# W_Q's load in two parts, of 16 and of 112 partitions, in a decode step on one core

## The chip, the cores and the metric

The kernel runs on one core of a Trainium2 chip. The metric is the device time of one execution in microseconds. Beside it there is the profile of one execution, taken by the hardware profiler: a span from the first to the last instruction, the busy time of each engine, and the packets that the core's 16 DMA engines moved. Engines are named as the profile names them: PE (TensorE's matmuls), PEld (its weight loads), DVE (VectorE), ACT (ScalarE), POOL (GpSimd), SP (SyncE, which only issues DMAs and waits here). SPq and ACTq are the DMA issues of SP and ACT.

## The reference

One decode step: four tokens (batch 4, one position, width 512) go through a layernorm and then, in parallel, through a sliding window attention over a cache and through a gated feed-forward block. All inputs are bf16.

```
xn = layernorm(x)                                   # 4 x 512
q  = xn @ wq                                        # 32 heads of 128
k, v = the last 4096 positions of the caches        # 8 key heads, each for 4 query heads
a  = softmax(q k^T / sqrt(128)) v @ wo
b  = (silu(xn @ w_gate) * (xn @ w_up)) @ w_down     # 1792 wide
out = x + a + b
```

The keys and values that are read make 32 MB each, W_Q and W_O 4 MB each, and the three matrices of the feed-forward block 1.75 MB each: 81.01 MB in all for one step of four tokens.

## The kernel before, in words

The program is written out by hand, engine by engine, with semaphores between the engines; nothing is planned by a scheduler.

**Loads.** SP issues nearly all of them, in one fixed order (L240 to L254): W_Q (L240), the keys of units 0 and 1 (`load_k`, L226), W_gate (L243), W_up (L244), the values of unit 0 (`load_v`, L230), then keys and values in turn, W_down (L249), the last values in two halves (L234), and W_O in five pieces (L238). A unit is one key head for two of the four batch rows: 4096 positions twice over, 2 MB of keys and 2 MB of values, so there are 16 units. Every load that SP issues into the chip's memory goes over 128 partitions: W_Q as 128 rows of 32 KB, a unit of keys as 128 rows of 16 KB. The loads of W_Q, keys 0 and 1, W_gate and W_up wait for nothing; the values of unit d wait until PE has finished with the values of the unit before (`s_pv`, L229), and the keys of unit d until unit d - 2 has been transposed (`s_tr`, L225). Two buffers stand for the keys and two for the values. ACT issues the load of x (L258), 4 rows of 1 KB.

**Start.** ACT and DVE make the layernorm from x; PE transposes it (L361) and DVE copies it out (L283). PE then waits for W_Q on the semaphore `d_wq` (L365) and computes q in 32 matmuls (L372, which stand in the profile under the helper's line, L356). They take W_Q by column blocks: every one of them reads all 128 partitions. DVE transposes q (L286) and spreads it out for the units (L289).

**Loop.** Eight passes over two units each (L432). In each half PE waits for the keys (`d_k`, L437), transposes them in groups of eight blocks (L384), and DVE copies each group out of PSUM (L298); PE multiplies them with q (L394), a row maximum is taken and subtracted (L303, L308, L404), ACT takes the exponential (L269), and PE multiplies with the values (L418). DVE normalizes the result (L312).

**End.** After the loop PE computes the feed-forward block's two first products (L454), the last values, the product with W_down (L466), and the product with W_O, piece by piece as its five loads land (L176). The result is copied out by DVE and ACT (L488, L490) and stored by SP (L492).

A load increments its semaphore by 16 when all of it has landed. Two loads on one semaphore are both complete at 32.

Of the kernel before, what the change touches and what calls it, by code (L numbers as in the profile page):

```python
# [10 lines left out]
def bass_parallel_sum__sliding_block_cached__swiglu_ffn__decode_kernel(  # L11
# [10 lines left out]
    out: bass.AP,  # L22
):
    B, _, D = A_x.shape
    _, HKV, Sk, Dh = A_k_cache.shape
    HQ = A_wq.shape[1] // Dh
    F = B_w_gate.shape[1]
# [25 lines left out]
    WQ = sb("wq_sb", [128, NC * HQ * Dh], BF16)  # L53
# [58 lines left out]
    def sem(name):  # L112
        return nc.alloc_semaphore(name=name)
    d_x = sem("d_x")
    d_wq = sem("d_wq")
# [44 lines left out]
    wq_ap = A_wq.rearrange("(p c) n -> p (c n)", c=NC)  # L160
# [6 lines left out]
    def kv_ap(cache, d):  # L167
        b0 = d % 2 * 2
        return cache[b0:b0 + 2, d // 2, Sk - W:, :].rearrange("b (q t) d -> q b (t d)", t=NT)
# [10 lines left out]
    with nc.Block() as block:  # L180
# [40 lines left out]
        @block.sync  # L221
        def _(eng):
            def load_k(d):
                if d >= 2:
                    eng.wait_ge(s_tr, 2 * NG * (d - 1))  # L225
                eng.dma_start(KB[:, d % 2 * KVN:(d % 2 + 1) * KVN], kv_ap(A_k_cache, d)).then_inc(d_k[d % 2], 16)  # L226

            def load_v(d):
                eng.wait_ge(s_pv, d + 1)  # L229
                eng.dma_start(VB[:, d % 2 * KVN:(d % 2 + 1) * KVN], kv_ap(A_v_cache, d)).then_inc(d_v[d % 2], 16)  # L230

            def load_v_half(d, h, done):
                a = d % 2 * KVN + h * HKN
                eng.dma_start(VB[:, a:a + HKN], kv_ap(A_v_cache, d)[:, :, h * HKN:(h + 1) * HKN]).then_inc(done, 16)  # L234

            def load_wo(n):
                a, b = WO_CUTS[n], WO_CUTS[n + 1]
                eng.dma_start(WO[:, a:b, :], wo_ap[:, a:b, :]).then_inc(d_wo[n], 16)  # L238

            eng.dma_start(WQ[:], wq_ap).then_inc(d_wq, 16)  # L240
            load_k(0)
            load_k(1)
            eng.dma_start(WG[:], wg_ap).then_inc(d_wg, 16)  # L243
            eng.dma_start(WU[:], wu_ap).then_inc(d_wu, 16)  # L244
            load_v(0)
            for d in range(2, ND):
                load_k(d)
                load_v(d - 1)
            eng.dma_start(WD[:], wd_ap).then_inc(d_wd, 16)  # L249
            eng.wait_ge(s_pv, ND)  # L250
            load_v_half(ND - 1, 0, d_v[1])
            load_v_half(ND - 1, 1, d_vz)
            for n in range(len(d_wo)):
                load_wo(n)  # L254
# [99 lines left out]
        def _(eng):  # L354
# [7 lines left out]
                                     xn[:].rearrange("b (p c) -> b c p", c=NC)[:, c, :], I4[:])  # L362
            last.then_inc(s_xT, 1)
            eng.wait_ge(s_xnT, 1)
            eng.wait_ge(d_wq, 16)  # L365

            for n in range(2):
                for c in range(NC):
# [153 lines left out]
```

## Time and profile before

| what | value |
|---|---|
| median of three runs | 196.37 us (196.15 to 196.51) |
| the profiled execution | 196.04 us |
| its span, first to last instruction | 194.8 us |
| mean granted clock of TensorE | 0.991 |
| bytes moved, mean rate over the span | 81.10 MB, 416 GB/s |
| busy time of PE, PEld, DVE, ACT, POOL | 162.8, 140.4, 114.9, 17.0, 10.3 us |
| W_Q from its issue to its landing | 12.4 us |

The busy times overlap, since the engines work side by side, and a busy PE is not a PE at its peak. "Idle before" in a row is the time an engine waited ahead of a group of instructions, with what ended it. The chain that ended last follows the work back from the last instruction, at each step to what released it. A window row gives the window, its length, the busy time of PE, PEld, DVE, ACT and POOL in it with the number of instructions, the granted clock, the share of time that the 16 DMA engines were busy, and the rate in GB/s; bytes count in the window in which their packet starts.

### The profile page before, as it was taken

The numbers are of one execution on the slowest core, as the hardware profiler recorded it, in microseconds if no ns is written. First come the engines' busy times: TensorE is split into PE (matmuls) and PEld (weight loads), VectorE is DVE, ScalarE is ACT, GpSimd is POOL, SyncE is SP. The second block draws the span as 40 slices with busy tenths as digits, with TensorE's granted clock in tenths as the row PEclk, the third lists the DMA queues.
The fourth block names the chain that finished last, engine by engine and source line by source line (L and its number), as shares of the span: only waits on it lengthen the run. The fifth ranks groups of instructions, "written<-read, shape, count | busy, mean of one in ns | idle before, by whom it ended". The sixth has DMA issues, their size and how long they took to land.

```text
span 194.8 us, 7757 instructions
## 1 busy us (share of the span) xinstructions
PE 162.8 (84%) x3465; PEld 140.4 (72%) x3466; DVE 114.9 (59%) x250; ACT 17.0 (9%) x27; POOL 10.3 (5%) x23
## 2 busy tenths in 40 slices
PE   0127999379898989898989898989898989898995
PEld 0113898378887888788878887888788878886752
DVE  1004777237676767676767676767676767675610
ACT  6600101001010101010101010101010101010100
POOL 8930000000000000000000000000000000000000
PEclk9999999879999999999999999999999999999999
DMA  6999999999999999999999999999999999999992
GB/s 216 431 431 431 434 421 434 422 431 431 431 431 431 434 427 431 434 431 434 434 431 431 431 431 434 431 431 431 431 431 431 431 431 431 431 433 417 439 401 105
DMA packets 6070, 81.10 MB, mean 416 GB/s; under 512 B 680, under 2 KB 816, under 8 KB 1072
## 3 DMA queue, kind: packets, MB, share of 16 engines
q1 hardware_dynamic: 6056, 81.01, 97.7%
q8 instruction: 5, 0.08, 0.1%
q14 instruction: 1, 0.01, 0.0%
q10 hardware_dynamic: 8, 0.00, 0.0%
HBM read 81.01 MB, written 0.00 MB: 416 GB/s over the span
## 4 chain that ended last, share of the span: by engine, by line
DMA 63%; PE 32%; issue 1%; DVE 1%; SPq 1%; DVEq 0%
DMA kbuf<-in_A_k_cache_dram 48%; PE ps_kt L384 16%; DMA wo_sb<-in_A_wo_dram 9%; PE ps_s L356 8%; DMA wq_sb<-in_A_wq_dram 6%; PE ps_o L356 5%; PE ps_kt L356 2%; PE ps_acc L176 1%; PE ps_acc L356 1%; DVE kT L298 1%; SPq L234 1%; DVE kT L286 0%; SPq L238 0%; DVE y_sb L488 0%; DVE qz L289 0%
## 5 line engine op out<-in xcount | busy, mean ns | idle before, releaser
L298 DVE COPY kT<-ps_kt 128x1024 bf16<-128x1024 bf16 x128 | 79.5, 684 | 24.8 <-PE ps_kt L384 24.8
L384 PE MATMUL ps_kt<-ident,kbuf 128*128 128x128 bf16 x1024 | 62.7, 219 | 10.2 <-DMA kbuf<-in_A_k_cache_dram 10.2
L384 PEld LDWEIGHTS ps_kt<-ident,kbuf 128*128 128x128 bf16 x1024 | 57.3, 98 | 15.3 <-issue 15.3
L356 PE MATMUL ps_o<-p,vbuf 128*128 128x64 bf16 x1120 | 39.2, 195 | 0.0
L356 PEld LDWEIGHTS ps_o<-p,vbuf 128*128 128x128 bf16 x1120 | 36.0, 99 | 1.1
L356 PEld LDWEIGHTS ps_s<-qz,kT 128*128 128x128 bf16 x1024 | 32.0, 99 | 6.7 <-issue 3.6
L356 PE MATMUL ps_s<-qz,kT 128*128 x1024 | 35.3, 193 | 1.2
L303 DVE TENSOR_REDUCE rm<-ps_s 128x8 bf16<-128x512 f32 x17 | 11.8, 692 | 23.9 <-PE ps_s L356 23.9
L269 ACT ACTIVATE p<-ps_s 128x512 bf16<-128x512 f32 x17 | 10.2, 597 | 162.4 <-PE ps_s L356 162.4
L356 PE MATMUL ps_o<-p,ones 128*128 128x128 bf16 (+1 forms) x69 | 7.0, 224 | 4.5 <-DMA vbuf<-in_A_v_cache_dram 3.1
L356 PEld LDWEIGHTS ps_o<-p,ones 128*128 128x128 bf16 x69 | 4.6, 99 | 5.6 <-DMA vbuf<-in_A_v_cache_dram 3.3
L356 PE MATMUL ps_kt<-wq_sb,xnT 128*32 128x512 bf16 x32 | 3.6, 629 | 5.7 <-DMA wq_sb<-in_A_wq_dram 5.7
L356 PE MATMUL ps_s<-dg,ones 8*128 8x512 bf16 x17 | 6.5, 385 | 0.0
L356 PE MATMUL ps_s<-mkc,mkr 2*128 2x512 bf16 x17 | 6.5, 385 | 0.0
L361 PE MATMUL ps_acc<-i,xn 4*128 4x4 f32 x4 | 0.6, 254 | 7.0 <-ACT xn L266 7.0
L356 PEld LDWEIGHTS ps_kt<-wq_sb,xnT 128*32 128x32 bf16 x32 | 1.2, 138 | 7.2 <-issue 7.2
L286 DVE STREAM_TRANSPOSE kT<-ps_kt 128x512 f32<-128x512 f32 x2 | 1.4, 718 | 8.4 <-PE ps_kt L356 8.4
L361 PEld LDWEIGHTS ps_acc<-i,xn 4*128 4x128 f32 x4 | 0.6, 206 | 7.0 <-issue 7.0
L314 DVE TENSOR_REDUCE den<-ps_o 128x8 f32<-128x128 f32 x18 | 4.9, 274 | 1.0 <-PE ps_o L356 1.0
L216 POOL MEMSET vbuf<- 128x6144 f32 x1 | 5.2, 5223 | 0.0
L308 DVE TENSOR_REDUCE m<-ps_acc 8x1 f32<-8x128 f32 x17 | 4.6, 270 | 0.3 <-PE ps_acc L356 0.3
L318 DVE TENSOR_TENSOR oT<-ps_o,den 128x8 f32 (+1 forms) x18 | 3.0, 167 | 2.9 <-issue 2.7
(68 smaller groups left out, 50.1 us busy)
## 6 DMA issues: line engine op xcount, KB each, us to landing
kbuf<-in_A_k_cache_dram SPq DMA_DIRECT2D x16, 2048.0 KB, 12.6
vbuf<-in_A_v_cache_dram SPq DMA_DIRECT2D x15, 2048.0 KB, 11.3
wq_sb<-in_A_wq_dram SPq DMA_DIRECT2D x1, 4096.0 KB, 12.4
vbuf<-in_A_v_cache_dram SPq DMA_DIRECT2D x2, 1024.0 KB, 9.2
wo_sb<-in_A_wo_dram SPq DMA_DIRECT2D x1, 2048.0 KB, 14.6
wg_sb<-in_B_w_gate_dram SPq DMA_DIRECT2D x1, 1792.0 KB, 25.7
wu_sb<-in_B_w_up_dram SPq DMA_DIRECT2D x1, 1792.0 KB, 29.3
wd_sb<-in_B_w_down_dram SPq DMA_DIRECT2D x1, 1792.0 KB, 15.0
```

What stands on the lines that cost most here:

```text
L176: last = eng.matmul(ps_acc[64 * n:64 * n + B, 0:256], OP[:, c, :], WO[:, c, 256 * n:256 * n + 256], start=False, stop=True, skip_group_che ...
L216: eng.memset(VB[:, HKN:].bitcast(FP32), 0.0)
L234: eng.dma_start(VB[:, a:a + HKN], kv_ap(A_v_cache, d)[:, :, h * HKN:(h + 1) * HKN]).then_inc(done, 16)
L269: eng.activation(P[:, d % 2 * PS:d % 2 * PS + SN], ps_S[d % 2][:], ACT.Exp, scale=SCALE).then_inc(s_p, 1)
L286: eng.transpose(qT[:, 512 * n:512 * n + 512], ps_kt[n][:])
L298: eng.tensor_copy(KT[:, u * HKN + 1024 * g:u * HKN + 1024 * (g + 1)], kt_ps[g].rearrange("p a b -> p (a b)")).then_inc(s_ev, 1)
L303: eng.tensor_reduce(RM[:], ps_S[bank][:].rearrange("p (t c) -> p c t", c=C), AX.X, ALU.max).then_inc(s_rm, 1)
L308: eng.tensor_reduce(m8[:], mt_ps, AX.X, ALU.max)
L314: eng.tensor_reduce(den[:], den_ps.rearrange("p (t c) -> p c t", c=C), AX.X, ALU.add)
L318: eng.tensor_tensor(OT[:, 2 * b:2 * b + 2, ds(r * REP, REP)], O_ps.rearrange("p (j h) -> p j h", j=2), den[:].rearrange("p (j h) -> p j h" ...
L356: return eng.matmul(o, l, r, start=start, stop=stop, skip_group_check=True)
L384: last = eng.transpose(kt_ps[g][:, k, :], KB[:, a:a + 128], ident[:])
```

## The change

W_Q comes in two loads, the first into partitions 0 to 15, the second into partitions 16 to 127. Both are issued by SP, one behind the other, at the place of the one load, and both increment `d_wq`, so PE waits for 32 in place of 16. Source rows, destination rows and everything else stay as they were; lines behind the load move down by two.

```diff
-            eng.dma_start(WQ[:], wq_ap).then_inc(d_wq, 16)
+
+            eng.dma_start(WQ[0:16, :], wq_ap[0:16, :]).then_inc(d_wq, 16)
+            eng.dma_start(WQ[16:128, :], wq_ap[16:128, :]).then_inc(d_wq, 16)
             load_k(0)
             load_k(1)
             eng.dma_start(WG[:], wg_ap).then_inc(d_wg, 16)
...
             eng.wait_ge(s_xnT, 1)
-            eng.wait_ge(d_wq, 16)
+            eng.wait_ge(d_wq, 32)
```

## The prediction

> **What bounds the kernel now.** I read the page first, from its slices down to the chain that ended last.
>
> ```profile
> span 194.8 us, 7757 instructions
> ...
> DMA  6999999999999999999999999999999999999992
> GB/s 216 431 431 431 434 421 434 422 431 431 431 431 431 434 427 431 434 431 434 434 431 431 431 431 434 431 431 431 431 431 431 431 431 431 431 433 417 439 401 105
> ...
> q1 hardware_dynamic: 6056, 81.01, 97.7%
> ...
> DMA 63%; PE 32%; issue 1%; DVE 1%; SPq 1%; DVEq 0%
> DMA kbuf<-in_A_k_cache_dram 48%; PE ps_kt L384 16%; DMA wo_sb<-in_A_wo_dram 9%; PE ps_s L356 8%; DMA wq_sb<-in_A_wq_dram 6%; PE ps_o L356 5%; PE ps_kt L356 2%; PE ps_acc L176 1%; PE ps_acc L356 1%; DVE kT L298 1%; SPq L234 1%; DVE kT L286 0
> ```
>
> Each digit is a fortieth of the span. Behind the first slice the DMA engines are full until the last, and the rate stands at 431 GB/s whichever tensor is loaded. 81.01 MB at 431 GB/s are 188.0 us of the 194.8. Next, windows over the start, the loop and the end; the last two columns are the DMA share and GB/s.
>
> ```profile
> 1.80:13.20 11.40, 0.61 (x4) 0.55 (x4) 1.14 (x4) 5.80 (x8) 9.10 (x13) 1.00 1.01 408
> ...
> 52.00:110.00 58.00, 53.59 (x1194) 48.00 (x1194) 39.46 (x85) 3.58 (x6) 0.00 (x0) 1.00 1.01 431
> 110.00:168.00 58.00, 53.55 (x1194) 47.99 (x1194) 39.47 (x84) 3.58 (x6) 0.00 (x0) 1.00 1.01 431
> 168.00:191.00 23.00, 20.74 (x416) 15.91 (x417) 12.30 (x31) 1.45 (x3) 0.00 (x0) 1.00 0.99 419
> ```
>
> The transfers never pause, so time lost at the start is not won back: what comes after W_Q needs the same number of us whenever it begins. PE is busy too, 53.6 us of 58, but it is PE that waits for the keys, by the list of waits, and for W_Q once:
>
> ```profile
> PE ps_kt L384 <- DMA kbuf<-in_A_k_cache_dram: 10.2, 14, 1.1
> ...
> PE ps_kt L356 <- DMA wq_sb<-in_A_wq_dram: 5.7, 1, 5.7
> ```
>
> The profiled execution took 196.04 us, 1.24 outside the span; the median is 196.37, 0.33 above it. The differences below are worked out on the span and added to the median.
>
> **The change part by part.** W_Q is on the path from its issue on, by the chain in order of time:
>
> ```profile
> 0.80 12.38 DMA wq_sb<-in_A_wq_dram
> ...
> 13.31 3.63 PE ps_kt L356 x32
> ```
>
> PE waits at the projection for all of it, before and after (16 counts become 32, both loads). Behind that wait stand the projection, DVE's two transposes, the first key transposes and, through them, SP's first value load.
>
> *Issue.* The timeline has the queues:
>
> ```profile
> 0.80 0.55 ACTq L258 DMA_DIRECT2D x_sb<-in_A_x_dram  x1
> ...
> 0.80 0.41 SPq L240 DMA_DIRECT2D wq_sb<-in_A_wq_dram  x1
> ...
> 1.26 1.34 SPq L226 DMA_DIRECT2D kbuf<-in_A_k_cache_dram  x2
> ...
> 2.64 0.59 SPq L243 DMA_DIRECT2D wg_sb<-in_B_w_gate_dram  x1
> ...
> 21.94 0.55 SPq L230 DMA_DIRECT2D vbuf<-in_A_v_cache_dram  x1
> ```
>
> One more issue takes 0.41 to 0.59 us of SP, so the second part of W_Q is issued at about 1.3 and K0, K1, W_gate and W_up each come some 0.5 us later. That is hidden: they queue behind W_Q, whose data run until about 12.9. It also bounds what a small first load saves at issue: four rows of x took 0.55 us, 128 rows of W_Q 0.41, so the issue does not shrink with the rows. K0, K1, W_gate and W_up make, with W_Q, 12.1 MB, or 28 us at 431 GB/s; the value load is issued at 21.94, long before they run out near 30. That cover of some 7 us stays, because the value load and the end of the queue move together.
>
> *Start of the data.* Windows of 0.1 and 0.2 us, which count a row of 32 KB in the window where it starts:
>
> ```profile
> 1.70:1.80 0.10, 0.00 (x0) 0.00 (x0) 0.00 (x0) 0.10 (x1) 0.10 (x2) 1.00 0.09 31
> 1.80:1.90 0.10, 0.00 (x0) 0.00 (x0) 0.00 (x0) 0.10 (x1) 0.10 (x2) 1.00 5.09 1321
> ...
> 2.20:2.30 0.10, 0.00 (x0) 0.00 (x0) 0.08 (x1) 0.10 (x1) 0.09 (x1) 1.00 4.05 1311
> 2.30:2.40 0.10, 0.00 (x0) 0.00 (x0) 0.10 (x1) 0.10 (x1) 0.10 (x2) 1.00 0.00 0
> ```
>
> ```profile
> 3.40:3.60 0.20, 0.00 (x0) 0.00 (x0) 0.00 (x0) 0.20 (x1) 0.20 (x2) 1.00 0.00 0
> 3.60:3.80 0.20, 0.00 (x0) 0.00 (x0) 0.00 (x0) 0.13 (x2) 0.20 (x1) 1.00 1.55 655
> ...
> 4.20:4.40 0.20, 0.00 (x0) 0.00 (x0) 0.00 (x0) 0.20 (x2) 0.20 (x3) 1.00 0.77 328
> 4.40:4.60 0.20, 0.00 (x0) 0.00 (x0) 0.13 (x1) 0.18 (x2) 0.20 (x2) 1.00 0.00 0
> ...
> 8.40:8.60 0.20, 0.00 (x0) 0.00 (x0) 0.00 (x0) 0.00 (x0) 0.20 (x1) 1.00 0.76 328
> ...
> 9.60:9.80 0.20, 0.00 (x0) 0.00 (x0) 0.00 (x0) 0.00 (x0) 0.20 (x1) 1.00 0.76 328
> ```
>
> Sixteen first rows, as many as there are engines, start between 1.8 and 2.3, the second sixteen between 3.6 and 4.4; later rounds are 1.2 us apart (the wave of 8.4 returns at 9.6). So the first round costs its latest engine 4.4 - 1.8 - 1.2 = 1.4 us above a clean one. That is the most a better start could give back: the bound below nothing is -1.4 us. I take 0 of it: the issue rows give no reason for an earlier start, and I know none for a quicker first row.
>
> *The second load's own cost.* It adds one more end of a load between two rows of each engine. The slices bound it: every 2 MB load of keys and values ends so, and the stream keeps 431 GB/s, against a best of 434 (439 once); 1 to 2% of a 4.9 us load is under 0.1 us. I take 0.
>
> *Where the rows land.* This is the term that decides. At 431 GB/s each engine moves 26.9 GB/s, 1.22 us for a row of W_Q; eight rounds are 9.7 us. All big loads here write 128 partitions, eight to an engine, so the trace cannot tell whether 26.9 GB/s is what an engine can carry or what a sixteenth of SBUF's partitions can take in. The first new load puts 512 KB into 16 neighbouring partitions.
> - If the engine is the limit: sixteen rows, one to an engine, 1.22 us, then seven rounds: 9.7 us as before, cost 0. That is the lower end.
> - If the partitions are, and the sixteenths are blocks of eight: two blocks with eight rows each, 9.7 us, while the engines, each stuck on its row, can't serve the other fourteen; these then need their own eight rows, 9.7 us. Together 19.4, cost +9.7. That is the upper end. (If the 16 rows went to two engines alone, these would have 8 + 7 rows, +8.5, inside it.)
> - Between: the sixteenths interleave, and 16 neighbours fall into four. Four rows deep, 4.9 us, and the untouched twelve still need 9.7: 14.6, cost +4.9. More if the 112 rows, seven to an engine, straddle sixteenths of eight so that engines wait for each other.
>
> I take the partitions as the limit: rows of 32 KB in W_Q and of 16 KB in the keys flow at the same rate within some 1%, so it is no engine's cost per row that sets it, and what all loads share is the flow into SBUF, eight partitions to a sixteenth. It is a lean, not a proof. Of the price I take the middle of +4.9 and +9.7, because the second load's sevens do straddle: **+7.3 us**.
>
> [...]
>
> *What is late next.* W_Q lands 7.3 us later, PE projects at 20.6 instead of 13.3, SP's first value load goes out at 29.2, and the stream that follows is the same 431 GB/s. Nothing behind it can absorb the delay: PE's idle in the loop is waiting for this same stream. The sum is 196.37 + 7.3 = 203.7 (196.04 + 7.3 = 203.3 for an execution like the profiled one).
>
> **The rivals.**
> 1. *No cost: the engines are the limit.* For it: the window at 1.70 holds 31 GB/s for 0.1 us, three of x's four rows of 1 KB; they go into four neighbouring partitions at more than 26.9, though so few bytes may sit in a buffer. It decides at one point: whether sixteen rows into 16 neighbours last 1.2 us or 4.9 and more. It gives 196.4, 196.0 to 196.8.
> 2. *A better start, the other side.* With engines as the limit, and one descriptor each in the first load, the first round loses part of its excess: 0.6 us for its earliest engine (3.6 - 1.8 - 1.2), 1.4 for its latest. Against it: issue time does not go by rows, and a first row needs its latency in any case. From -0.4 to the bound of -1.4: 195.0 to 196.0; with half of the 1.4, 195.7.
> 3. *Shared at a higher rate.* A sixteenth takes two engines at full speed: the four-deep round takes 2.4 us for 1.2, +1.2: 197.6 (to +4.9, 201.2).
> 4. *Every round collides.* If the 112 rows are handed out in turn, each round of sixteen is again sixteen neighbours: 8 x 4.9 = 38.9 us for 9.7, +29.2: 225.6. Against it: the one-load form shows no such collision at all, so somebody hands its rows out with care.
> 5. *The change does nothing*, since both parts run as one stream: same time and the same evidence as rival 1.
>
> **How the numbers follow.** A run of this kernel can tell 0.2%, 0.4 us, from no change. Whether engine or partitions bind, the rows leave open; but a gain has only 1.4 us to draw on, with a reason against it, and a loss has several ways that all cost over 1 us. Partitions bind, +4.9 to +9.7: 0.62. Rival 3: 0.08. Rival 4: 0.07. Rivals 1 and 5: 0.13. Rival 2: 0.10. Slower is 0.62 + 0.08 + 0.07 = 0.77; same 0.12 and faster 0.11, with a hundredth of rival 1 lying faster. The likeliest case alone spans 201.2 to 206.1. The range takes in rivals 1 and 3 and leaves out 2 and 4 (0.17): 195.9 to 206.3.
>
> **What would show it.** Right: windows of the changed kernel from 1.8 on show some 50 to 110 GB/s for 5 to 10 us, then an uneven stretch; the wait at L356's counterpart for wq_sb grows from 5.7 to about 13 us, the projection starts near 20.6, and the loop runs at 431 GB/s as before. Issue right: SP's K0 half a microsecond later and nothing else moved by it. Wrong: second rows starting at 3.6 to 4.4 again and the projection at 13.3 (rival 1); at 12 to 13 (rival 2); a stretch of about 100 GB/s over 39 us (rival 4). A later W_Q with an end that did not move by as much would refute that the stream passes every delay on.

## The result and the profile after

The changed kernel takes 205.05 us (median of five runs, 204.64 to 205.19) beside 196.37 us for the kernel before (five runs, 196.12 to 196.71): a ratio of 1.0442, 95% interval 1.0422 to 1.0461. It is 8.7 us slower; the forecast was 203.7 us, 7.3 us slower. The profiled execution took 205.1 us with a span of 203.8.

From the page of the changed kernel: the 40 slices, the DMA queue and the chain that ended last.

```profile
span 203.8 us, 7759 instructions
...
DMA  8999999999999999999999999999999999999992
GB/s 117 193 309 228 367 421 430 438 418 426 434 428 440 428 428 437 421 437 428 434 434 428 428 437 424 444 428 428 437 421 437 428 434 434 428 428 421 434 408 94
...
q1 hardware_dynamic: 6072, 81.01, 97.7%
...
DMA 63%; PE 32%; issue 1%; DVE 1%; SPq 1%; DVEq 0%
DMA kbuf<-in_A_k_cache_dram 44%; PE ps_kt L386 17%; DMA wq_sb<-in_A_wq_dram 10%; DMA wo_sb<-in_A_wo_dram 8%; PE ps_s L358 7%; PE ps_o L358 5%; PE ps_kt L358 2%; PE ps_acc L176 1%; PE ps_acc L358 1%; DVE kT L300 1%; SPq L234 1%; DVE kT L288 0%; SPq L238 0%; DVE y_sb L490 0%; SPq L241 0%
```

The row to compare is the rate. In the kernel before it stood at 431 from the second slice on; here it needs five slices, 25 us, to get there. Behind them nothing has changed. The DMA digits hide this: they say 8 and 9 while the rate is half. From 4.90 to 20.20 us the DMA share is 0.98 at 240 GB/s, below, and in the kernel before it is 1.00 at 432. A full DMA share is not a full rate.

Windows of the changed kernel, with the rate in the last column, over the first load, the second load, and the stream behind them:

```profile
1.80:4.90 3.10, 0.00 (x0) 0.00 (x0) 0.68 (x1) 1.48 (x2) 2.83 (x11) 1.00 1.19 169
4.90:20.20 15.30, 0.61 (x4) 0.55 (x4) 0.47 (x3) 4.31 (x7) 6.26 (x3) 1.00 0.98 240
...
60.00:110.00 50.00, 46.71 (x1060) 41.96 (x1057) 34.30 (x73) 2.98 (x5) 0.00 (x0) 1.00 1.01 432
```

The same for the kernel before, whose first rows start in the first window and the other seven rounds in the second:

```profile
1.80:3.60 1.80, 0.00 (x0) 0.00 (x0) 0.67 (x1) 1.54 (x2) 1.53 (x8) 1.00 1.08 292
3.60:12.10 8.50, 0.61 (x4) 0.55 (x4) 0.47 (x3) 4.26 (x7) 7.57 (x6) 1.00 1.00 432
```

The sixteen first rows hold the engines for 3.1 us in place of 1.8 before any second row starts, and the 112 rows of the second load go at 240 GB/s in place of 432: 15.3 us for 8.5. By these windows the first load costs 1.3 us and the second 6.8; the other 1.2 of the delay below is the tail of W_Q, which lands 2.3 us behind the second window in place of 1.1. The larger part of the loss is the second load's. What follows from it is in the waits and the chain in order of time:

```profile
PE ps_kt L358 <- DMA wq_sb<-in_A_wq_dram: 13.6, 1, 13.6
```

```profile
0.80 0.40 SPq L241
1.19 0.06 issue
1.25 21.25 DMA wq_sb<-in_A_wq_dram
22.50 0.14 issue
22.64 3.63 PE ps_kt L358 x32
```

The projection starts at 22.64, 9.33 us later than in the kernel before; the span is 203.8 for 194.8, 9.0 longer. Nearly all of the delay reaches the end.

### The profile page after: what moved, and what is told of

It is laid out like the page before. It is cut to its first block, busy times and chain, and to the rows that moved or that the text cites. A ratio compares the mean times of both kernels' runs of the same rounds, so it can differ in the third digit from the quotient of the medians.

```text
span 203.8 us, 7759 instructions
## 1 busy us (share of the span) xinstructions
PE 164.7 (81%) x3466; PEld 141.6 (69%) x3466; DVE 115.4 (57%) x250; ACT 17.0 (8%) x27; POOL 10.3 (5%) x23
## 4 chain that ended last, share of the span: by engine, by line
DMA 63%; PE 32%; issue 1%; DVE 1%; SPq 1%; DVEq 0%
DMA kbuf<-in_A_k_cache_dram 44%; PE ps_kt L386 17%; DMA wq_sb<-in_A_wq_dram 10%; DMA wo_sb<-in_A_wo_dram 8%; PE ps_s L358 7%; PE ps_o L358 5%; PE ps_kt L358 2%; PE ps_acc L176 1%; PE ps_acc L358 1%; DVE kT L300 1%; SPq L234 1%; DVE kT L288 0%; SPq L238 0%; DVE y_sb L490 0%; SPq L241 0%
## 5 line engine op out<-in xcount | busy, mean ns | idle before, releaser
L386 PE MATMUL ps_kt<-ident,kbuf 128*128 128x128 bf16 x1024 | 65.4, 224 | 11.0 <-DMA kbuf<-in_A_k_cache_dram 10.7
L386 PEld LDWEIGHTS ps_kt<-ident,kbuf 128*128 128x128 bf16 x1024 | 59.7, 100 | 16.3 <-issue 16.3
L358 PE MATMUL ps_o<-p,vbuf 128*128 128x64 bf16 x1120 | 38.7, 194 | 0.0
L358 PEld LDWEIGHTS ps_s<-qz,kT 128*128 128x128 bf16 x1024 | 31.4, 98 | 6.6 <-issue 3.6
L358 PE MATMUL ps_s<-qz,kT 128*128 x1024 | 34.7, 192 | 1.2
L358 PE MATMUL ps_kt<-wq_sb,xnT 128*32 128x512 bf16 x32 | 3.6, 629 | 13.6 <-DMA wq_sb<-in_A_wq_dram 13.6
L363 PE MATMUL ps_acc<-i,xn 4*128 4x4 f32 x4 | 0.6, 254 | 8.4 <-ACT xn L268 8.4
L363 PEld LDWEIGHTS ps_acc<-i,xn 4*128 4x128 f32 x4 | 0.6, 206 | 8.4 <-issue 8.4
L176 PE MATMUL ps_acc<-wo_sb,oP 128*4 128x256 bf16 x64 | 4.0, 272 | 0.8 <-DMA wo_sb<-in_A_wo_dram 0.8
```

Of the source, the lines that this page charges most:

```text
L176: last = eng.matmul(ps_acc[64 * n:64 * n + B, 0:256], OP[:, c, :], WO[:, c, 256 * n:256 * n + 256], start=False, stop=True, skip_group_che ...
L358: return eng.matmul(o, l, r, start=start, stop=stop, skip_group_check=True)
L363: last = eng.transpose(xT_ps[:, c * B:(c + 1) * B], xn[:].rearrange("b (p c) -> b c p", c=NC)[:, c, :], I4[:])
L386: last = eng.transpose(kt_ps[g][:, k, :], KB[:, a:a + 128], ident[:])
```

## The experiments

The last column of a window row is again the rate. "Behind W_up" means that an extra load comes where the stream runs at 431 GB/s; PE then starves for a while and, in these kernels, its granted clock falls to about half (0.50 to 0.52 over 6 to 12 us of each; 0.72 in the kernel before, from 36.40 to 42.40 us), so the total can hold more than the extra load's time (17.0 us for 14.9 with the 112 rows) and the windows are read first. Extra loads go into W_O's buffer (`WOF` is that buffer with 16,384 columns); SP waits for them before W_O itself is loaded. The diffs show the lines of the loads alone: as in the changed kernel, the semaphore count that PE waits for goes by the number of W_Q's loads, 32 for two and 128 for eight.

### Two loads by columns

```diff
+            eng.dma_start(WQ[:, 0:2048], wq_ap[:, 0:2048]).then_inc(d_wq, 16)
+            eng.dma_start(WQ[:, 2048:16384], wq_ap[:, 2048:16384]).then_inc(d_wq, 16)
```

> W_Q in two loads by columns, an eighth and seven eighths of every row, both over 128 partitions. Theory P (what is slow is many engines writing into few partitions): no cost, 196.4 us within 0.4, second rows as early as in the kernel before, projection near 13.3 us. Theory L (a second load on the queue, or its issue and completion, is what costs): about the 205 us of the changed kernel.

Measured: 196.46 us, ratio 1.0024 (1.0008 to 1.0041). P stands, L falls. W_Q comes even a little earlier (the projection of this kernel, in the timeline):

```profile
12.96 3.60 PE L357 MATMUL ps_kt<-wq_sb,xnT 128*32 128x512 bf16 x32 [5.09 <-DMA wq_sb<-in_A_wq_dram]
```

0.35 us earlier at the projection, and nothing of it is left at the end. So this small first load, with 429 GB/s from 3.60 to 12.10 us, is no gain either, and a second load as such costs at most some 0.4 us (0.8 by the upper end of the interval).

### The first load alone, to neighbours and spread out

```diff
+            eng.dma_start(WOF[0:16, :], wq_ap[0:16, :]).then_inc(d_ex, 16)
             eng.dma_start(WQ[:], wq_ap).then_inc(d_wq, 16)
```

> W_Q whole as before, and ahead of it an extra load of its first 16 rows (512 KB) into partitions 0 to 15 of W_O's buffer, which is filled later; nothing reads the extra rows. It prices the first load alone. Theory P: its 16 rows take 3 to 4.3 us each as in the changed kernel, then eight clean rounds of 1.2 us: W_Q lands 3.4 to 4 us later than before, 199.8 to 200.4 us. If the first load were most of the 8.7 us: 203 us and more. Theory L: 205 us.

The second kernel writes the same source rows elsewhere:

```diff
+            eng.dma_start(WOF[0:106:7, :], wq_ap[0:16, :]).then_inc(d_ex, 16)
             eng.dma_start(WQ[:], wq_ap).then_inc(d_wq, 16)
```

> As e2_near, the same 16 source rows, but into the partitions 0, 7, 14 to 105. Theory P: the extra rows take 1.5 to 2.6 us as a first round of W_Q before did, W_Q lands 1.2 to 2.4 us later than before, 197.6 to 198.8 us. Theory S (reading 16 neighbouring rows of the source is what is slow, wherever they go): as e2_near.

Measured: 199.81 us, ratio 1.0187 (1.0168 to 1.0206), and 198.32 us, ratio 1.0104 (1.0084 to 1.0125), beside 196.04 for the kernel before. The issue lists, size and us to landing, for the neighbours first and the spread rows second:

```profile
wq_sb<-in_A_wq_dram SPq DMA_DIRECT2D x1, 4096.0 KB, 15.7
...
wo_sb<-in_A_wq_dram SPq DMA_DIRECT2D x1, 512.0 KB, 6.6
```

```profile
wq_sb<-in_A_wq_dram SPq DMA_DIRECT2D x1, 4096.0 KB, 14.0
wo_sb<-in_A_wq_dram SPq DMA_DIRECT2D x1, 512.0 KB, 5.2
```

Same bytes from the same source: where they land makes 1.5 us of difference, so theory S falls for the first load. 3.8 us for an extra load whose bytes alone take 1.2 at 431 GB/s leaves 2.5 us for what the first load costs where its bytes are no extra. A part of that falls on the round behind it, the first of the whole W_Q, which takes 2.55 us in place of 1.2:

```profile
5.20:7.75 2.55, 0.61 (x4) 0.55 (x4) 0.15 (x1) 2.30 (x4) 2.55 (x2) 1.00 0.90 206
```

Of the 8.7 us, some 6 are then the second load's by subtraction. The windows above draw the line at the start of the second rows, and give it 6.8 and the late landing.

### Eight loads of 16

```diff
+            for p in range(0, 128, 16):
+                eng.dma_start(WQ[p:p + 16, :], wq_ap[p:p + 16, :]).then_inc(d_wq, 16)
```

> W_Q in eight loads of 16 partitions. Theory P: every round of sixteen rows meets in 16 neighbouring partitions, 3.7 to 4.9 us for each, 30 to 39 us in place of 9.7: 216 to 226 us. Theory L with a cost per load of 8.7 us: 257 us; with one of 0.5 us: 200 us.

Measured: 222.04 us, ratio 1.1323 (1.1302 to 1.1345), inside P. Its windows over rounds two to eight, and behind them:

```profile
5.20:36.70 31.50, 0.61 (x4) 0.55 (x4) 0.33 (x2) 2.99 (x4) 6.10 (x2) 1.00 1.01 117
...
39.00:60.00 21.00, 19.59 (x334) 14.98 (x335) 12.83 (x28) 0.61 (x2) 0.00 (x0) 1.00 1.01 431
```

Seven rounds in 31.5 us are 4.5 us each. 117 GB/s is what sixteen neighbouring partitions take in, 27% of 431, a little over four sixteenths, which would be 108.

### Halves: neighbours, and even and odd

```diff
+            eng.dma_start(WQ[0:64, :], wq_ap[0:64, :]).then_inc(d_wq, 16)
+            eng.dma_start(WQ[64:128, :], wq_ap[64:128, :]).then_inc(d_wq, 16)
```

> [...] The steady round of 16 neighbours in e4_sixteens took 4.5 us, 116 GB/s, four times 29. Theory P with shares that take 29 GB/s and two engines on each (0 to 31 and 32 to 63 on the same eight shares): 2.25 us in each of the eight rounds, 18 us for 9.7: 204 to 205 us. With shares of eight partitions each to itself, all sixteen over two loads: the same. Theory T (only a load into very few partitions is slow): 196 to 197 us.

```diff
+            for p in range(2):
+                eng.dma_start(WQ[p:128:2, :], wq_ap[p:128:2, :]).then_inc(d_wq, 16)
```

> W_Q in two loads of 64 rows, the even and the odd partitions. Each load reaches every sixteenth of the partitions. If what counts is which shares a load reaches in all: no cost, 196 to 197 us. If what counts is how many engines stand on one share at the same moment (each engine has four rows in turn, 2 partitions apart, and engines 4 apart meet in every round): 2.25 us a round, as e5_halves, 204 to 205 us.

Measured: 206.5 us, ratio 1.0506 (1.0483 to 1.0528), somewhat above the range of P; and 196.41 us, ratio 1.0013 (0.9995 to 1.003). Windows of the two, neighbours first:

```profile
3.90:21.50 17.60, 0.61 (x4) 0.55 (x4) 0.47 (x3) 4.21 (x6) 7.25 (x6) 1.00 1.01 209
```

```profile
4.00:12.50 8.50, 0.61 (x4) 0.55 (x4) 0.47 (x3) 3.96 (x6) 7.15 (x6) 1.00 1.00 432
```

The same number of loads, of rows and of bytes, at about half the rate or at the full one. Of the two theories for the even rows the first, that the shares reached in all count, gives the rate of this load; the second, with engines that meet in every round, falls. That an engine gets four rows in turn was my assumption, which no run shows; it, or what I took a meeting to cost, is wrong for this load, and I know no better one from these runs.

### The second load alone, and two loads of rows 7 partitions apart

```diff
             eng.dma_start(WU[:], wu_ap).then_inc(d_wu, 16)
+            eng.dma_start(WOF[16:128, :], wq_ap[16:128, :]).then_inc(d_ex, 16)
```

> The kernel before with an extra load of 112 rows of W_Q (3.67 MB) into partitions 16 to 127 of W_O's buffer, issued behind W_up, where the stream runs steadily; nothing reads it. It prices the second load without the first. Clean, it would take 8.5 us: 204.6 us. Theory C (in every round some engines meet on a share, and all sixteen wait for them): seven rounds of 2.0 to 2.25 us, 14 to 16 us, 210 to 212 us, all engines together. Theory I (only the engines that meet wait; sevens in order over shares of eight at 29 GB/s, followed by hand): the engines end spread from 8.5 to 12.3 us, 208.3 us.

```diff
             eng.dma_start(WU[:], wu_ap).then_inc(d_wu, 16)
+            for h in (0, 8192):
+                eng.dma_start(WOF[0:106:7, h:h + 8192], wq_ap[0:16, h:h + 8192]).then_inc(d_ex, 16)
```

> The kernel before with two extra loads behind W_up, each of 16 rows of 16 KB into partitions 0, 7, 14 to 105 of W_O's buffer; nothing reads them. [...] Clean: 0.61 us a round, 197.4 us. [...]

Measured: 213.13 us, ratio 1.0827 (1.0776 to 1.0879), and 199.33 us, ratio 1.0131 (1.0103 to 1.0159). Windows of the first, before the 112 rows, over them, and after:

```profile
25.00:30.40 5.40, 5.32 (x122) 4.95 (x119) 3.24 (x6) 0.60 (x1) 0.00 (x0) 1.00 1.01 428
30.40:45.30 14.90, 7.39 (x118) 6.20 (x114) 6.05 (x13) 0.60 (x1) 0.00 (x0) 0.69 1.04 249
45.30:48.20 2.90, 0.00 (x0) 0.00 (x0) 0.00 (x0) 0.00 (x0) 0.00 (x0) 0.50 0.88 288
48.20:60.00 11.80, 4.26 (x73) 4.18 (x74) 0.69 (x1) 0.00 (x0) 0.00 (x0) 0.50 1.00 426
```

The 112 rows alone, in a steady stream and with no small load ahead, go at 249 GB/s, as they do in the changed kernel (240). That is the second load's cost shown by itself: some 15 us for 8.5. The total is above both theories; PE, starved, runs at half its clock (the 0.50 ahead of the last two columns) and must catch up. The windows fit C better: 14.9 us lie in its 14 to 16, where theory I ended at 12.3. Three single rounds from the middle, each of sixteen rows of 32 KB (0.52 MB), show the same:

```profile
36.37:38.73 2.36, 1.33 (x13) 1.33 (x14) 0.69 (x1) 0.00 (x0) 0.00 (x0) 0.50 0.94 222
38.73:40.66 1.93, 1.84 (x18) 1.57 (x15) 1.45 (x4) 0.00 (x0) 0.00 (x0) 0.50 1.12 272
40.66:43.02 2.36, 0.00 (x0) 0.00 (x0) 0.64 (x1) 0.00 (x0) 0.00 (x0) 0.50 0.99 222
```

Each takes about 2 us, none 1.2; by theory I the engines that meet nobody would run ahead. Windows of the second kernel, before, over, and after its two extra loads:

```profile
28.00:30.60 2.60, 2.60 (x57) 2.23 (x54) 2.60 (x6) 0.00 (x0) 0.00 (x0) 1.00 1.03 433
30.60:33.50 2.90, 2.90 (x60) 2.53 (x60) 1.71 (x7) 0.60 (x1) 0.00 (x0) 1.00 1.01 274
33.50:36.30 2.80, 0.51 (x10) 0.34 (x7) 1.70 (x3) 0.00 (x0) 0.00 (x0) 1.00 0.97 263
36.30:48.00 11.70, 5.65 (x86) 5.57 (x87) 1.38 (x2) 0.00 (x0) 0.00 (x0) 0.52 1.02 432
```

For 5.7 us the rate is 269 GB/s, that is 1.5 MB, although the extra loads hold 0.5 MB: the first value rows behind them, laid over 128 partitions, are slowed with them. The loss is (431 - 269) / 431 of 5.7 us, 2.1 us, where the clean case had none. So the slow rate outlasts the extra rows: 263 GB/s from 33.50 to 36.30 us. Why rows 7 partitions apart are slow here at all is not shown.

### Which side decides

```diff
             eng.dma_start(WU[:], wu_ap).then_inc(d_wu, 16)
+            eng.dma_start(WOF[0:128:2, :], wq_ap[0:64, :]).then_inc(d_ex, 16)
```

> The kernel before with an extra load of 64 rows (2 MB) behind W_up: the neighbouring source rows 0 to 63 of W_Q into the even partitions of W_O's buffer; nothing reads it. If the destination decides: clean as in e6_evenodd, 431 GB/s, 4.9 us more, 201 us. If reading neighbouring rows is what slowed e5_halves: about 204 GB/s, 10.3 us more, 206 us and what PE loses while it starves.

```diff
             eng.dma_start(WU[:], wu_ap).then_inc(d_wu, 16)
+            eng.dma_start(WOF[0:64, :], wq_ap[0:128:2, :]).then_inc(d_ex, 16)
```

> As e9_64spread with the two sides exchanged: the even source rows into the neighbouring partitions 0 to 63. If the destination decides: about 204 GB/s as in e5_halves, 10.3 us, 206 us and what PE loses while it starves. If the source decides: 431 GB/s, 201 us.

Measured: 200.87 us, ratio 1.0245 (1.0223 to 1.0268), and 208.04 us, ratio 1.062 (1.0582 to 1.0657). One window of each, spread destination first:

```profile
30.10:40.00 9.90, 5.94 (x121) 5.03 (x117) 5.94 (x14) 0.60 (x1) 0.00 (x0) 0.95 1.00 424
```

```profile
30.10:40.00 9.90, 4.21 (x89) 3.29 (x86) 3.28 (x9) 0.60 (x1) 0.00 (x0) 0.77 1.04 228
```

Neighbouring source rows into spread partitions are clean (424 GB/s), and spread source rows into neighbouring partitions are not (228). The destination decides, for these 64 rows.

### Eight loads of every eighth partition

```diff
+            for p in range(8):
+                eng.dma_start(WQ[p:128:8, :], wq_ap[p:128:8, :]).then_inc(d_wq, 16)
```

> W_Q in eight loads of 16 rows, each into every eighth partition (p, p + 8, to p + 120). Theory G (groups of four neighbouring partitions, 32 of them, each take 29 GB/s): every row has a group for itself, 196 to 197 us. Theory S (sixteen shares, partitions 32 apart share one): two engines meet on each of eight shares, 2.25 to 2.57 us a round, 18 to 20.6 us for 9.7: 204 to 206.5 us. In e4_sixteens, neighbours: 222 us.

Measured: 206.64 us, ratio 1.0533 (1.0514 to 1.0553). Its window over rounds two to eight:

```profile
4.00:20.00 16.00, 0.61 (x4) 0.55 (x4) 0.47 (x3) 3.93 (x6) 7.15 (x6) 1.00 1.09 225
```

About half the rate, 225 GB/s for 432: G falls, S stands (a hair above its range). Sixteen rows 8 partitions apart, each in a group of four to itself, are still slow. Two engines on each of eight shares would fit this; which partitions share one is not shown.

### The first load alone, in the steady stream

```diff
             eng.dma_start(WU[:], wu_ap).then_inc(d_wu, 16)
+            eng.dma_start(WOF[0:16, :], wq_ap[0:16, :]).then_inc(d_ex, 16)
```

> The kernel before with an extra load of 16 rows (512 KB) into partitions 0 to 15 of W_O's buffer behind W_up, where no first round hides a part of it. At the steady 4.5 us of e4_sixteens: 116 GB/s for 4.5 us, 200.5 us and what PE loses while it starves. At the head of the queue the same load cost 3.8 us (e2_near), so 0.7 us or more would be what the slow first round covers there. If less than 3.8 us here: the head of the queue has a cost of its own.

Measured: 201.91 us, ratio 1.0288 (1.0266 to 1.0311), 5.9 us more than the kernel before. Windows of this kernel over the extra rows, and behind them:

```profile
30.10:35.00 4.90, 3.94 (x75) 3.08 (x70) 3.59 (x10) 0.60 (x1) 0.00 (x0) 1.00 1.15 182
35.00:40.00 5.00, 0.00 (x0) 0.00 (x0) 0.23 (x1) 0.00 (x0) 0.00 (x0) 0.65 0.89 283
```

Against 431 GB/s the two windows lack 2.8 and 1.7 us, 4.5 together, and the extra rows' own bytes take 1.2: 5.8 us of stream, where 4.5 was expected. The load disturbs the rows behind it here too. At the head of the queue the same load cost 3.8. At most 1.4 of these 2 us can lie under the excess that the first round has in any case; where the rest comes from is not shown.

## Why the prediction was right, point by point

- **The bound.** Right. The stream runs at 432 GB/s behind W_Q as before and passes the delay on: 9.33 us at the projection, 9.0 at the end. One size was off: the first value load was forecast for 29.2 and goes out at 33.00, 11.06 us later than before, so the cover ahead of it is 1.7 us thinner than it was. The stream does not run dry: 429 GB/s from 30 to 60 us.

```profile
33.00 0.54 SPq L230 DMA_DIRECT2D vbuf<-in_A_v_cache_dram  x1
```

- **The issue.** Right. The timeline of the changed kernel has the second part of W_Q at 1.25 and the keys at 1.70 (1.26 before), and nobody waits for it:

```profile
1.25 0.40 SPq L242 DMA_DIRECT2D wq_sb<-in_A_wq_dram  x1
1.70 1.85 SPq L226 DMA_DIRECT2D kbuf<-in_A_k_cache_dram  x2
```

- **The start.** Right that a small first load gains nothing: in the split by columns 0.35 us are gained at the projection and none at the end. Rivals 1 and 2 fall with the split by columns and with the two kinds of halves, where a load of the same rows and bytes runs at 209 or at 432 GB/s.
- **The second load's own cost.** Right within the measure: two loads of even and odd partitions cost 0.13% (-0.05 to 0.3).
- **Where the rows land.** That partitions bind and not engines was right, and is shown: the destination decides for 16 rows (1.5 us) and for 64 (424 or 228 GB/s), and sixteen neighbours take in 117 GB/s, four sixteenths, as the middle case had it. The reason given for it was no reason: rows of 32 and of 16 KB at one rate fit an engine limited by its bytes just as well. The terms were mis-sized against each other. Of the +4.9 of the middle case 3.7 are the first load's (4.9 for 1.2), and 1.2 are the second's, by eight rows in place of seven in each untouched sixteenth (9.7 for 8.5); seven clean rounds would have left +3.7. Straddling added the 2.4 from +4.9 to the middle, so the second load stood at 3.6. It cost some 6 by subtraction, and the first load 2.5 at the head of the queue; in the steady stream, where no slow first round is there, the windows lack 4.5. The two errors partly cancel, which left 1.35 us between 203.7 and 205.05. That is luck in the number: one of the two bounds, blocks of eight neighbours, falls with the 117 GB/s of sixteen neighbours (two sixteenths would be 54), so the middle was taken between a case that holds and one that does not. That the 112 rows are slow was foreseen; that straddling makes them slow is not shown, and rows behind a crowded load are slow too (283 GB/s behind the 16 neighbours in the steady stream), which the forecast did not have.
- **The signs.** The wait for W_Q (13.6 us for about 13) and the loop's rate came as named. The first stretch did not: 50 to 110 GB/s for 5 to 10 us were named, and the windows have 169 for 3.1 us and then 240 for 15.3. Most of the loss sits in that long stretch; the forecast had it half and half (3.7 and 3.6).
- **Rival 3** (a share takes two engines at full speed) falls with the neighbouring halves at 209 GB/s and with every eighth partition at 225.
- **Rival 4** did not happen, but its price was right: in eight loads of 16 every round collides, and 222 us was measured for 225.6. The 112 rows are not handed out in that way: 240 GB/s, not 117.

What stays open is how 112 rows are dealt to the engines, and why their rounds take about 2 us in place of 1.2. If sixteen neighbours lie in four sixteenths of the partitions, as their 117 GB/s fits, these hold sixteen more, so that partitions 16 to 127 still reach all sixteen, as the even partitions do; they run at 249 GB/s against 432, and reaching all is then not enough. That it is the place that slows these 112 rows is taken over from the 16 and the 64: no run put 112 rows at other places, so a cost of that shape itself is not excluded. By either division of the forecast (sixteenths of eight neighbours, or interleaved ones) the clean loads (128 rows, the even, the odd ones) have as many rows in every sixteenth as in every other, and the 112 rows do not. This is argued, not shown, since the profile does not say which engine moved which row.

No version here beats the kernel before; its one load over 128 partitions already runs at 432 GB/s from its second round on.

## What to carry to other kernels

The rate of W_Q's loads went by where their rows land, 432 GB/s for the even partitions and 209 for neighbouring halves: before cutting a load by partitions, time each part's rate in windows; cut by columns if it must be cut, which cost 0.24% here. Read the rate and not the DMA share, which stood at 0.98 here at 240 GB/s. A small head start is worth no more than the excess of the first round, 1.4 us here, and a load that breaks the layout can cost several times that: 8.7 us in this change, and 5.9 for 16 neighbours in the steady stream, where the rows behind them went at 283 GB/s.

## What the runs showed of the hardware that was not expected

- The even partitions alone, or the odd ones, load at 432 GB/s, the neighbouring halves at 209: here a load need not span 128 rows to be fast.
- Slowness spreads. Two extra loads of 16 rows into partitions 0, 7, 14 to 105 cost 2.1 us of stream beside 1.2 us for their bytes' own time, or 3.2 us in the total, and slowed the value rows behind them (263 GB/s from 33.50 to 36.30 us).
- A small load of another queue came later as well. The load of x, 4 KB, issued by ACT, was awaited 2.2 us in the kernel before and 3.6 in the changed one; the layernorm came 1.35 us later (L363 at 8.38, L361 at 7.03 before), hidden under W_Q. The row of the changed kernel's groups:

```profile
L278 DVE TENSOR_REDUCE st_neg<-x_sb 4x1 f32<-4x512 bf16 x1 | 0.7, 675 | 3.6 <-DMA x_sb<-in_A_x_dram 3.6
```
